# First x tiles of a two-branch kernel loaded and turned by pairs of 128-feature chunks, with extra warm-up matmuls and pinned parameter turns

## The chip, the cores and the metric

The kernel runs on one core of a Trainium2 chip. The metric is the device time of one execution in microseconds (us). PE is TensorE's matmul side, PEld its weight loads, DVE is VectorE, ACT is ScalarE, SP is the queue that issues most DMAs.

Three measures are used side by side: the timed runs; the profile's timeline of TensorE; and the completion records of the trace, which give for each DMA the moment at which each of the 16 DMA engines reported its share as landed. A time "landed at 15.03" is the last of the 16. All times inside a run count from the start of its span.

## The reference, cut to what matters

Two independent branches, each over 2048 tokens of 1024 features, are concatenated. Branch A is a complex state-space scan. Branch B is segment-wise attention of 32 heads with a memory carried from segment to segment. Only the start of B's value projection matters here:

```python
v = jnp.einsum('btd,dhe->bhte', h, Wv)      # h: (memory and) tokens x 1024, Wv: 1024 x 32 x 128
```

The kernel computes it in blocks of four heads (512 columns of Wv). The weights of block 0 are called wv0 below, those of block 1 wv1, 1 MB each.

## The kernel before: the parts that the change and the argument touch

The value matmuls of this kernel contract over the partitions, so x (tokens by features) must be turned to features by tokens. For the first 512 tokens this is done on TensorE (a matmul with the identity into a PSUM buffer, then a VectorE copy from there to SBUF); the other 1536 tokens use transposing loads. The split is meant to avoid transposing loads that arrive too late; the first of them was issued from 11.27 us in the kernel before and landed at 20.03. In the profile lines below a_hs is the SBUF buffer that x's rows and the weights are loaded to, b_xe holds the turned x, and psO, psS and psP are buffers in PSUM.

```python
    def load_rows(self, t, xr, e, cs=slice(0, D)):
        self.k.tc.keep_in_program_order(e.dma_start(xr[:, t, cs], self.x[0][t * 128 + 64:t * 128 + 192, cs]))

    def turn_rows(self, t, xr):
        k = self.k
        pt = k.ps("O", (128, 2, 1024), BF16)
        for c in range(KC):                                   # KC = 8 chunks of 128 features
            k.tc.keep_in_program_order(k.PE.transpose(pt[...], xr[:, t, c * 128:(c + 1) * 128], k.ident[:]))
        for i in range(2):
            k.copy("v", self.xe[:, 4 * i:4 * i + 4, t * 128:(t + 1) * 128], pt[:, i, 0:512]...)

    def v_first(self, w, xr, e):                              # block 0, tokens 0 to 511
        p = [k.ps("A") for t in range(4)]
        for t, todo in enumerate((((0, 0, 2),), ((0, 2, 4), (1, 0, 4)), ((0, 4, 6), (1, 4, 6), (2, 0, 6)),
                                  ((0, 6, 8), (1, 6, 8), (2, 6, 8), (3, 0, 8)))):
            self.turn_rows(t, xr)
            for tt, c0, c1 in todo:
                self.v_mm(p[tt], tt, w, range(c0, c1))        # 128 x 512 matmuls, one per chunk
        ...                                                   # evacuation by ScalarE, store
# ---- in kernel_main
            q2 = (k.SP, nc.scalar)                            # two issuing queues
            for t in range(4):
                for j in range(2):
                    b.load_rows(t, xr, q2[j], slice(j * 512, j * 512 + 512))      # 128 KB each
                for j in range(2):
                    b.load_wv(0, wvs[0], KC, q2[j], [2 * t + j])                  # 128 KB each
            for j in range(2):
                b.load_wv(1, wvs[1], 2, q2[j], [j])           # wv1: two halves of 512 KB
            a.load_params(tmp)                                # three loads of 2 KB
            k.SP.dma_start(tmp[0:M, 0:D], b.mem0[0])          # 16 KB
            b.load_x(512, 1024); b.load_x(1024, 1536); b.load_x(1536, T)          # transposing loads
            ...
            for i in range(7):                                # warm-up
                k.PE.matmul(pw[:, i % 2, :], one[:, 0:128], one, start=True, stop=True)
```

After block 0's four tiles TensorE goes on with the first four tiles of block 1, which need wv1; in the middle of them it turns the parameters (nine small matmuls). The loads take their completion semaphores in turn from a set of eight (numbers 100 and 103 to 109 here), and from the ninth load on each issue waits for the semaphore that it is to use, that is for the load eight before it. The ninth was issued at 3.42 us, the first had landed at 3.40.

## Time and profile before

| | before |
|---|---|
| time, median of all its runs in the first comparison | 1242.95 us (1242.38 to 1243.32, 6 runs) |
| span of the profiled run | 1240.8 us |
| PE busy | 1234.9 us |
| block 1 (wv1) starts | 15.07 us |
| last 32 matmuls start | 1235.23 us |

First the page: the span, and busy time (share of the span) and instructions of each engine. Then the list of who PE waited for in the whole run (total us, times, longest).

```profile
span 1240.8 us, 19711 instructions
...
PE 1234.9 (100%) x8148; PEld 655.2 (53%) x8148; DVE 611.2 (49%) x1124; ACT 325.9 (26%) x754; POOL 199.9 (16%) x284
```

```profile
PE psO L913 <- PEq L1118: 0.9, 1, 0.9
PE psO L379 <- DMA a_hs<-in_B_x_dram: 0.6, 1, 0.6
PE psS L414 <- DVE b_xe L77: 0.5, 1, 0.5
PE psS L414 <- DMA a_hs<-in_B_Wv_dram: 0.2, 1, 0.2
```

TensorE is the bottleneck, and all its listed waits lie in the first 15.1 us. The PE timeline of that stretch (start, busy time, line, operation, how many; in brackets the idle time before and what ended it; L379 are the turns, L414 the value matmuls; the last line, L718, is the kernel's last 32 matmuls):

```profile
3.79 1.06 PE L379 MATMUL psO<-ident,a_hs 128*128 128x128 bf16 x8
5.37 0.64 PE L414 MATMUL psS<-a_hs,b_xe 128*128 128x512 bf16 x2 [0.52 <-DVE b_xe L77]
6.59 0.62 PE L379 MATMUL psO<-ident,a_hs 128*128 128x128 bf16 x8 [0.58 <-DMA a_hs<-in_B_x_dram]
...
12.96 1.89 PE L414 MATMUL psP<-a_hs,b_xe 128*128 128x512 bf16 x8
15.07 1.90 PE L414 MATMUL psS<-a_hs,b_xe 128*128 128x512 bf16 x8 [0.22 <-DMA a_hs<-in_B_Wv_dram]
...
1235.23 1.95 PE L718 MATMUL psP<-b_xe,b_ol 128*128 128x128 bf16 x32
```

The 0.52 us is the wait for VectorE's copy of the first turned tile, the 0.58 us the wait for the second x tile. The last eight matmuls of block 0 start at 12.96 us; eight take 1.73 us (start to start), so block 0 is through at 14.69 us. Block 1 starts at 15.07 us. The completion records say why:

```
landed at (us)      x tile 0   wv0 c0,1   x tile 1   wv0 c2,3   x tile 2   wv0 c4,5   x tile 3   wv0 c6,7      wv1 halves
kernel before       3.59       4.92       6.55       7.28       7.82       8.58       9.52       11.42         15.03 (first), 14.84
```

wv1's first half lands 0.04 us before its first matmul. Between 9 and 10 us the DMAs move only 171 GB/s (332 between 5 and 7 us).

### The profile page before, as it was taken

What the parts mean: (1) busy time and instruction counts of PE and PEld (TensorE: products, weight loads), DVE (VectorE), ACT (ScalarE), POOL (GpSimd) and SP (SyncE); (2) the same over time, 40 slices, a digit from 0 to 9 for tenths busy, and PEclk for the clock granted to TensorE, in tenths of its full rate; (3) what the DMA queues carried; (4) which work ended last, traced back from release to release, by engine and by line L of the source; (5) the groups of instructions that cost most, each with busy time, mean ns of one, the idle gap of its engine ahead of it and who ended that gap; (6) DMA issues with size and microseconds to landing.
All of it is one profiled execution on the core that took longest, in us unless ns stands there. A gap on an engine that the chain in (4) does not pass through costs nothing.

```text
span 1240.8 us, 19711 instructions
## 1 busy us (share of the span) xinstructions
PE 1234.9 (100%) x8148; PEld 655.2 (53%) x8148; DVE 611.2 (49%) x1124; ACT 325.9 (26%) x754; POOL 199.9 (16%) x284
## 2 busy tenths in 40 slices
PE   9999999999999999999999999999999999999998
PEld 4444444444455445566666655655565554454444
DVE  4889999999941222444444444444444550011000
ACT  3344434444310001333333323333333230000000
POOL 2000000000032140222222222232222330000000
PEclk9999999999999999999999999999999999999999
DMA  9942232332566558577668554645575469607000
GB/s 223 260 130 68 85 94 68 102 94 77 153 189 202 158 161 170 100 151 150 138 122 173 123 136 95 129 77 103 106 139 106 72 203 231 140 18 153 17 18 28
DMA packets 306056, 153.95 MB, mean 124 GB/s; under 512 B 147242, under 2 KB 299810, under 8 KB 305962
## 3 DMA queue, kind: packets, MB, share of 16 engines
q1 hardware_dynamic: 304138, 150.82, 52.6%
q10 hardware_dynamic: 1824, 1.84, 0.5%
q8 instruction: 65, 1.06, 0.4%
q14 instruction: 29, 0.24, 0.1%
HBM read 73.70 MB, written 44.71 MB: 95 GB/s over the span
## 4 chain that ended last, share of the span: by engine, by line
PE 98%; DMA 1%; DVE 0%; issue 0%
PE psP L585 33%; PE psS L685 9%; PE psO L256 9%; PE psS L414 9%; PE psP L414 9%; PE psP L685 5%; PE psS L310 4%; PE psP L310 4%; PE psP L568 4%; PE psO L629 3%; PE psS L611 3%; PE psO L685 2%; PE psS L718 1%; PE psP L505 1%; PE psP L737 1%; PE psO L482 1%
## 5 line engine op out<-in xcount | busy, mean ns | idle before, releaser
L585 PE MATMUL psP<-b_xe,w 128*128 128x480 bf16 x2048 | 439.6, 366 | 0.0
L585 PEld LDWEIGHTS <-w 128*128 128x128 bf16 x2048 | 193.7, 98 | 183.5
L618 POOL TENSOR_TENSOR b_m<-b_e,maskB 99x396 bf16<-99x396 bf16 x160 | 139.4, 871 | 348.2 <-ACT b_e L614 348.2
L77 DVE CAST b_q<-psP 128x480 bf16<-128x480 f32 (+1 forms) x192 | 98.1, 532 | 145.4 <-PE psP L585 133.9
L414 PEld LDWEIGHTS <-b_xe 128*128 128x128 bf16 x1024 | 99.8, 98 | 121.3 <-DVE b_xe L77 1.1
L75 ACT ACTIVATE b_k<-psP 128x480 bf16<-128x480 f32 x128 | 73.1, 571 | 319.1 <-PE psP L585 319.1
L685 PEld LDWEIGHTS <-b_ol 128*128 128x128 bf16 x960 | 93.1, 98 | 109.3
L614 ACT ACTIVATE b_e<-psS 99x396 bf16<-99x396 f32 x176 | 87.4, 497 | 170.9 <-PE psS L611 165.5
L636 DVE TENSOR_TENSOR b_ot<-psO,b_rall 99x512 bf16<-99x512 f32 x176 | 121.7, 692 | 6.4
L256 PE MATMUL psO<-w,a_bt 128*128 128x512 bf16 x512 | 115.7, 379 | 0.0
L634 DVE RECIPROCAL b_rall<-psO 99x4 f32<-99x4 f32 x176 | 31.3, 178 | 132.8 <-PE psO L629 132.8
L685 PE MATMUL psS<-w,b_ol 128*128 128x512 bf16 x416 | 92.1, 379 | 0.0
L414 PE MATMUL psS<-w,b_xe 128*128 128x512 bf16 x384 | 90.7, 379 | 0.0
L414 PE MATMUL psP<-w,b_xe 128*128 128x512 bf16 x384 | 90.7, 379 | 0.0
L256 PEld LDWEIGHTS <-a_bt 128*128 128x128 bf16 x512 | 49.7, 98 | 59.0
L310 PEld LDWEIGHTS <-a_hs 128*128 128x128 bf16 x512 | 49.5, 98 | 58.3
L77 DVE CAST b_ost<-psS 128x512 bf16<-128x512 f32 x13 | 9.0, 692 | 125.4 <-PE psS L685 125.4
L629 PE MATMUL psO<-b_v,b_m 99*128 99x129 bf16 x704 | 70.4, 221 | 0.0
L611 PEld LDWEIGHTS <-b_k 128*128 128x128 bf16 x704 | 50.0, 98 | 33.9 <-DVE b_k L77 0.2
L611 PE MATMUL psS<-b_q,b_k 128*128 128x99 bf16 x704 | 60.1, 208 | 0.0
L75 ACT ACTIVATE b_vst<-psS 128x512 bf16<-128x512 f32 x56 | 33.4, 597 | 99.5 <-PE psS L414 75.6
L310 PE MATMUL psS<-w,a_hs 128*128 128x512 bf16 x256 | 57.9, 379 | 0.0
(203 smaller groups left out, 1097.9 us busy)
## 6 DMA issues: line engine op xcount, KB each, us to landing
b_v<-b_vx SPq DMA_DIRECT2D x16, 1056.0 KB
b_os<-b_ot SPq DMA_DIRECT2D x16, 960.0 KB
w<-in_B_Wv_dram SPq DMA_DIRECT2D x14, 1024.0 KB
b_vx<-b_vst SPq DMA_DIRECT2D x48, 256.0 KB
w<-in_B_Wo_dram SPq DMA_DIRECT2D x12, 1024.0 KB
w<-in_B_Wq_dram SPq DMA_DIRECT2D x16, 512.0 KB
w<-in_B_Wk_dram SPq DMA_DIRECT2D x16, 512.0 KB
a_xn<-in_A_x_dram SPq DMA_DIRECT2D x32, 128.0 KB
```

Of the source, the lines that this page charges most:

```text
L75: self.S.activation(out, in_, ACT.Copy)
L77: self.V.tensor_copy(out, in_)
L256: m = PE.matmul(u[:, i, :], self.bt[:, i, c, :], self.xT[tb][:, c, :], start=(c == 0), stop=(c == KC - 1))
L310: PE.matmul(py[:], self.hs[tb][:, pc, i, tt * 128:(tt + 1) * 128], self.ct[half, i][:, pc, :], start=(pc == 0 and i == 0), stop=(pc == PC ...
L414: m = self.k.PE.matmul(p[:], self.xe[:, c, t * 128:(t + 1) * 128], w[:, c, :], start=(c == 0), stop=(c == KC - 1))
L585: PE.matmul(p[:, 0:480], w[:, i * KC + c, hh * 128:(hh + 1) * 128], self.xe[:, c, 480 * q:480 * q + 480], start=(c == 0), stop=(c == KC - 1))
L611: PE.matmul(s[:, j * GW:(j + 1) * GW], kt[:, hh, g0:g0 + 128], qt[:, hh, g0:g0 + GW], start=True, stop=True)
L614: k.S.activation(e[:], s[0:GW, 0:4 * GW], ACT.Exp, scale=float(E) ** -0.5, accum_out=self.accE[0:GW, i:i + 1])
L618: k.G.tensor_tensor(v4(m[:, 0:4 * GW]), v4(e[:]), mask[0:GW, :, :].unsqueeze(2).to_broadcast([GW, 2, 2, GW]), ALU.mult)
L629: PE.matmul(o[:, gg, cs], m[:, j * GW:j * GW + 128], vt[:, 2 * u + gg, cs], start=True, stop=True)
L636: V.tensor_tensor(ot[:, 2 * u:2 * u + 2, :].rearrange("p g (h e) -> p g h e", h=2), oa[:, :, 1:257].rearrange("p g (h e) -> p g h e", h=2) ...
L685: k.PE.matmul(self.acc[t, half], ol[:, h8, tt * 128:(tt + 1) * 128], self.wo_half(half, h), start=(h == 0), stop=(h == H - 1))
```

## The change

Its intent: let TensorE start sooner and wait less in block 0. x comes in pieces of 256 tokens by 256 features (two chunks), each turned by four turns and one copy; the filler matmul of 384 columns covers the first copy; the warm-up is 256 columns longer. The turns of the parameters and of the initial memory get pins, so that the scheduler keeps them at their place in TensorE's order. Two side effects: each Wv chunk now goes to the queue that does not carry the x piece beside it, and the warm-up matmuls are pinned too and write to a psS buffer instead of psO.

```diff
-    def load_rows(self, t, xr, e, cs=slice(0, D)):
-        self.k.tc.keep_in_program_order(e.dma_start(xr[:, t, cs], self.x[0][t * 128 + 64:t * 128 + 192, cs]))
-    def turn_rows(self, t, xr):   # 8 turns, 2 copies (cut)
+    def load_rows(self, j, q, xr, e):
+        cs = slice(256 * q, 256 * q + 256)
+        self.k.tc.keep_in_program_order(e.dma_start(
+            xr[:, 2 * j:2 * j + 2, cs], self.x[0][256 * j + 64:256 * j + 320, cs].rearrange("(i p) d -> p i d", p=128)))
+    def turn_rows(self, j, q, xr, c0=0, n=2):   # 2 turns per chunk, 1 copy (cut)
@@ v_first
-        for t, todo in enumerate((((0, 0, 2),), ((0, 2, 4), (1, 0, 4)), ...)):   # cut
+        for c in range(2):
+            self.turn_rows(0, 0, xr, c, 1)
+        self.warm(384)
+        for q in range(4):
+            if q > 0:
+                self.turn_rows(1, q, xr)
+            for t in range(2):
+                self.v_mm(p[t], t, w, (2 * q,))
+            if q == 0:
+                self.turn_rows(1, q, xr)
+            for t in range(2):
+                self.v_mm(p[t], t, w, (2 * q + 1,))
+            if q < 3:
+                self.turn_rows(0, q + 1, xr)
+            for t in range(2, 4):
+                self.v_mm(p[t], t, w, range(2 * q, 2 * q + 2))
@@ kernel_main
-            for t in range(4):
+            for q in range(4):
                 for j in range(2):
-                    b.load_rows(t, xr, q2[j], slice(j * 512, j * 512 + 512))
-                for j in range(2):
-                    b.load_wv(0, wvs[0], KC, q2[j], [2 * t + j])
+                    b.load_rows(j, q, xr, q2[j])
+                    b.load_wv(0, wvs[0], KC, q2[1 - j], [2 * q + j])
-            for i in range(7):
-                k.PE.matmul(pw[:, i % 2, :], one[:, 0:128], one, start=True, stop=True)
+            for n in 7 * (512,) + (256,):
+                b.warm(n)                       # one pinned matmul of n columns; its definition is cut
@@ params, init
-        PE.matmul(pr[:, 0:3 * PC], r24, ...)
+        k.tc.keep_in_program_order(PE.matmul(pr[:, 0:3 * PC], r24, ...))          # and the same for mem0's turns
```

The bytes, the number of loads ahead of wv1 (16), the turns and the value matmuls are the same.

More of the change, by code (lines that the diff above doesn't have):

```diff
@@ L149, in params @@
         pr = k.ps("O")[:, 0, :]
-        PE.matmul(pr[:, 0:3 * PC], r24, k.ident[0:3 * PC, 0:3 * PC], start=True, stop=True)
+        k.tc.keep_in_program_order(PE.matmul(pr[:, 0:3 * PC], r24, k.ident[0:3 * PC, 0:3 * PC], start=True, stop=True))
         raw = pool.tile([128, 3, PC], FP32, name="a_raw", bufs=1)
@@ L343, in init @@
         for c in range(KC):
-            k.PE.matmul(pm[:, c * M:(c + 1) * M], tmp[0:M, c * 128:(c + 1) * 128], k.ident[0:M, 0:M], start=True, stop=True)
+            k.tc.keep_in_program_order(
+                k.PE.matmul(pm[:, c * M:(c + 1) * M], tmp[0:M, c * 128:(c + 1) * 128], k.ident[0:M, 0:M], start=True, stop=True))
         self.memT = self.xe[:, :, T:XE]
@@ L369, in load_x @@
                 k.SP.dma_start(self.xe[:, :, lo:hi], self.x[0][lo + r:hi + r, :], transpose=True)
-    def load_rows(self, t, xr, e, cs=slice(0, D)):
-        self.k.tc.keep_in_program_order(e.dma_start(xr[:, t, cs], self.x[0][t * 128 + 64:t * 128 + 192, cs]))
-    def turn_rows(self, t, xr):
-        k = self.k
-        pt = k.ps("O", (128, 2, 1024), BF16)
-        for c in range(KC):
-            k.tc.keep_in_program_order(k.PE.transpose(pt[:, c // 4, (c % 4) * 128:(c % 4) * 128 + 128], xr[:, t, c * 128:(c + 1) * 128], k.ident[:]))
-        for i in range(2):
-            k.copy("v", self.xe[:, 4 * i:4 * i + 4, t * 128:(t + 1) * 128], pt[:, i, 0:512].rearrange("p (c n) -> p c n", c=4))
+    def load_rows(self, j, q, xr, e):
[3 more added lines that the diff above has]
+    def turn_rows(self, j, q, xr, c0=0, n=2):
+        k = self.k
+        pt = k.ps("O", (128, 2, 256), BF16)
+        for c in range(n):
+            for i in range(2):
+                cs = 256 * q + 128 * (c0 + c)
+                k.tc.keep_in_program_order(k.PE.transpose(
+                    pt[:, c, i * 128:i * 128 + 128], xr[:, 2 * j + i, cs:cs + 128], k.ident[:]))
+        k.copy("v", self.xe[:, 2 * q + c0:2 * q + c0 + n, 256 * j:256 * j + 256], pt[:, 0:n, :])
     def sum_x(self, q, pool):
@@ L442, in v_pair, with warm @@
         yield
+    def warm(self, n):
+        k = self.k
+        one = k.nc.const_aps.tensor(1.0, [128, n], BF16)
+        k.tc.keep_in_program_order(k.PE.matmul(self.pw[:, 0, 0:n], one[:, 0:128], one, start=True, stop=True))
     def v_first(self, w, xr, e):
@@ L447, in v_first @@
         p = [k.ps("A") for t in range(4)]
-        for t, todo in enumerate((((0, 0, 2),), ((0, 2, 4), (1, 0, 4)), ((0, 4, 6), (1, 4, 6), (2, 0, 6)),
-                                  ((0, 6, 8), (1, 6, 8), (2, 6, 8), (3, 0, 8)))):
-            self.turn_rows(t, xr)
-            for tt, c0, c1 in todo:
-                self.v_mm(p[tt], tt, w, range(c0, c1))
+        for c in range(2):
[14 more added lines that the diff above has]
+                self.v_mm(p[t], t, w, range(2 * q, 2 * q + 2))
         for q in range(2):
@@ L909, in kernel_main @@
             b.load_x(1536, T)
-            one = nc.const_aps.tensor(1.0, [128, 512], BF16)
-            pw = k.ps("O")
-            for i in range(7):
-                k.PE.matmul(pw[:, i % 2, :], one[:, 0:128], one, start=True, stop=True)
+            b.pw = k.psp.tile([128, 1, 512], FP32, name="psS", bufs=2)
+            for n in 7 * (512,) + (256,):
+                b.warm(n)
             def values():
```

## The prediction

> **What bounds the kernel.** TensorE. The profile page has PE busy 1234.9 of 1240.8 us. The table of PE waits for the whole run lists four: 0.9 us before the first instruction, 0.6 us for a load of B's x, 0.5 us for VectorE's copy of the first turned tile, 0.2 us for Wv. All lie in the first 15.1 us. So the change can only move the moment from which PE runs without a gap: 15.07 us in the before timeline, where the second value block (weights wv1) starts.
>
> **What the change does.** Before, PE takes four 128-token tiles, 8 turns each; after, pieces of 256 tokens by 256 features (4 turns, one copy). Turns, matmuls and bytes stay the same. Added: 256 and 384 columns of warm-up. In the instruction order the pinned parameter turns keep their place on PE: worth 0.0 us. x loads become 512 B packets instead of 1024 B.
>
> **PE's side (estimate).** From the trace: a warm 512 matmul 0.216 us (8 in 1.73), a turn 0.055, cold 0.43 and 0.107; the copy of 512 columns 0.38 us. The first four turns start at 4.0 us (warm-up is 0.2 us longer), the filler hides the copies, the first value matmul starts about 4.8 instead of 5.37; a short wait for the second pieces at about 6.2 remains. v_first then ends near 13.6 us instead of 14.7: about 1.0 us gained. The clock should warm up at the same time (full rate from about 5.4 us before[...]).
>
> **DMA's side.** Completion records of the trace (last of 16 engines): x tile 0 at 3.6, wv0 chunks 0 and 1 at 4.9, x tile 1 at 6.55, chunks 2, 3 at 7.3, x tile 2 at 7.8, chunks 4, 5 at 8.6, x tile 3 at 9.5, chunks 6, 7 at 11.4, wv1's halves at 14.84 and 15.03. PE's 15.07 start is wv1's arrival: PE was already out of work at 14.7. The change doesn't touch wv1: it is issued behind the same 2 MB, with the same eight transfers in flight. So the 1.0 us becomes a longer wait for wv1 (about 1.3 us instead of 0.22).
>
> Smaller packets can make it later: median 27 ns per 512 B packet against 46 ns per 1024 B, so 1 MB of x costs (2048*27-1024*46)/16 = 0.5 us more engine time; DMA isn't saturated throughout (9 to 10 us moved only 171 GB/s), so I expect 0 to 0.4 us, against some luck in which engine straggles (wv0's last chunk had 15 of 16 engines done at 9.7 and the last at 11.25).
>
> **Critical path.** Of the 1.0 us on PE nearly nothing reaches the end. Expected: -0.7 to +0.5 us, centre -0.2 (0.1 by the DMA argument, shaded for a luckier landing of wv1).
>
> **Prediction.** 1242.9 us, 8 in 10 between 1242.1 and 1243.7; faster by over 2% 0.003, within 2% 0.994, slower 0.003.
>
> **What would show it.** Right: in the PE timeline the first block's matmuls end at 13 to 14 us; the waits list has a Wv wait over 1 us; the next block starts at 14.7 to 15.5; the copy wait is gone. Wrong: the second block starts before 14.3 us, or the first ends past 14.5.
>
> **What would make it wrong.** wv1 landing much earlier (fewer stragglers, or the x transposes of the SP queue starting later and contending less) would give up to 1.2 us; more contention[...] would cost 0.5 to 2 us.

That the clock would warm up at the same time as before (the trace's record has full rate from 5.48 us) was the estimate.

## The result, and the profile after

| | before | after |
|---|---|---|
| time, median (range, runs) | 1242.95 us (1242.38 to 1243.32, 6) | 1242.87 us (1241.89 to 1243.31, 6) |
| ratio, 95% interval | | 0.9999 (0.9986 to 1.0012) |
| block 0 through on PE | 14.69 | 13.93 |
| wv1's first half landed | 15.03 | 15.09 |
| block 1 starts | 15.07 | 15.13 |
| last 32 matmuls start | 1235.23 | 1235.30 |
| span | 1240.8 | 1240.9 |

Ratios are the mean time of one kernel's runs over that of the other's of the same rounds, so they are not quite the ratio of the medians. The page, the PE waits of the whole run, and the largest waits of the weight loads (PEld):

```profile
span 1240.9 us, 19646 instructions
...
PE 1231.7 (99%) x8080; PEld 655.7 (53%) x8150; DVE 611.2 (49%) x1125; ACT 326.2 (26%) x754; POOL 200.3 (16%) x284
```

```profile
PE psS L420 <- ACT a_hs L75: 1.0, 1, 1.0
PE psS L454 <- PEq L1139: 0.8, 1, 0.8
```

```profile
PEld L420 <- DMA a_hs<-in_B_Wv_dram: 1.5, 1, 1.5
```

(The trace of this run lacks 68 matmul records, 8080 against 8148; so its busy sum is not to be compared.) The PE timeline: L385 are the turns, L454 warm-up and filler, L420 the value matmuls, L741 the last 32 matmuls.

```profile
4.00 0.63 PE L385 MATMUL psO<-ident,a_hs 128*128 128x128 bf16 x4
4.43 0.53 PE L454 MATMUL psS<-const-bfloat16-1.0 128*128 128x384 bf16 x1
4.81 0.61 PE L420 MATMUL psS<-a_hs,b_xe 128*128 128x512 bf16 x1
...
13.50 0.59 PE L420 MATMUL psP<-a_hs,b_xe 128*128 128x512 bf16 x2
15.13 1.90 PE L420 MATMUL psS<-a_hs,b_xe 128*128 128x512 bf16 x8 [1.04 <-ACT a_hs L75]
...
1235.30 1.95 PE L741 MATMUL psP<-b_xe,b_ol 128*128 128x128 bf16 x32
```

Block 0 runs without the two waits of before and is through at 13.93 us (its last two matmuls start at 13.50 and take 0.216 us each), 0.76 us earlier. Then PE stands for 1.04 us (the timeline counts from the modelled end of the last matmul, 14.09 us) and starts block 1 at 15.13 us, as late as before. The timeline puts that wait down to ScalarE, the weight loads' list to the DMA of Wv. The records say the DMA: wv1's first half landed at 15.09 us.

### The profile page after: what moved, and what is told of

Its sections match the earlier page's. It is cut to its first block, busy times and chain, and to the rows that moved or that the text cites. A ratio compares the mean times of both kernels' runs of the same rounds, so it can differ in the third digit from the quotient of the medians.

```text
span 1240.9 us, 19646 instructions
## 1 busy us (share of the span) xinstructions
PE 1231.7 (99%) x8080; PEld 655.7 (53%) x8150; DVE 611.2 (49%) x1125; ACT 326.2 (26%) x754; POOL 200.3 (16%) x284
## 4 chain that ended last, share of the span: by engine, by line
PE 99%; issue 0%; ACT 0%; DVE 0%
PE psP L608 33%; PE psS L708 9%; PE psS L420 9%; PE psO L256 9%; PE psP L420 9%; PE psP L708 5%; PE psP L310 4%; PE psS L310 4%; PE psP L591 4%; PE psO L652 3%; PE psS L634 3%; PE psO L708 2%; PE psS L741 1%; PE psP L528 1%; PE psP L760 1%; PE psO L505 1%
## 5 line engine op out<-in xcount | busy, mean ns | idle before, releaser
L420 PEld LDWEIGHTS <-b_xe 128*128 128x128 bf16 x1024 | 99.7, 98 | 120.4 <-DMA a_hs<-in_B_Wv_dram 1.5
L420 PE MATMUL psS<-w,b_xe 128*128 128x512 bf16 x378 | 90.1, 379 | 0.4
L420 PE MATMUL psP<-w,b_xe 128*128 128x512 bf16 x376 | 89.8, 379 | 0.4
```

Of the source, the lines that this page charges most:

```text
L420: m = self.k.PE.matmul(p[:], self.xe[:, c, t * 128:(t + 1) * 128], w[:, c, :], start=(c == 0), stop=(c == KC - 1))
```

## The experiments

Every run's output was correct. Twelve kernels ran, all with five rounds, in three groups; the kernel before ran beside each group with medians of 1242.22 (11 runs), 1242.43 (9) and 1242.67 us (9). Because the intervals are about 0.0013 wide on either side (1.6 us), the timeline carries the verdicts. The table has for each profiled run when block 1 started, when the last 32 matmuls of the kernel started, the difference of the two, and what remained to the end of the span.

| run | loads ahead of wv1 | wv1 first half landed | block 1 starts | last 32 start | difference | rest to the end | DMAs against before |
|---|---|---|---|---|---|---|---|
| before | 16 | 15.03 | 15.07 | 1235.23 | 1220.16 | 5.60 | 0 |
| after | 16 | 15.09 | 15.13 | 1235.30 | 1220.17 | 5.60 | 0 |
| e1 after, no wv1 wait | 16 | (15.00) | 14.05 | 1234.29 | 1220.24 | | 0 |
| e2 before, no wv1 wait | 16 | (14.75) | 14.65 | 1234.79 | 1220.14 | | 0 |
| e3 after, late x | 16 | 15.46 | 15.50 | 1237.31 | 1221.81 | 6.13 | +1 |
| e4 after, fewer loads | 10 | 13.34 | 14.57 | 1234.72 | 1220.15 | 6.12 | -6 |
| e5 after, mixed loads | 12 | 14.50 | 14.54 | 1234.70 | 1220.16 | 5.91 | -4 |
| e6 before, mixed loads | 12 | 14.28 | 14.60 | 1234.75 | 1220.15 | 5.91 | -4 |
| e7 as e5, no extra warm-up | 12 | 13.89 | 14.30 | 1234.45 | 1220.15 | 5.91 | -4 |
| e8 after, no pins | 16 | 16.30 | 17.56 | 1239.00 | 1221.44 | 5.60 | 0 |
| e9 as e7, DMA count kept | 12 | 14.30 | 14.52 | 1234.67 | 1220.15 | 5.61 | 0 |
| e10 before, one DMA more | 16 | 15.78 | 15.83 | 1235.99 | 1220.16 | 6.14 | +1 |
| e11 before, mixed, count kept | 12 | 13.41 | 14.95 | 1235.11 | 1220.16 | 5.58 | 0 |
| e12 after, 11 loads, count kept | 11 | 13.80 | 14.97 | 1235.12 | 1220.15 | 5.56 | 0 |

The column "difference" is the main reading: except in e3 and e8 the work from block 1 to the last matmuls takes 1220.14 to 1220.24 us whatever the start was like. A gain or loss at 15 us arrives at the end of TensorE's work unchanged; nothing takes it back on the way.

Theory A: TensorE's gain in block 0 is eaten by the wait for wv1. Rival B: block 1 waits for ScalarE to free its PSUM bank, as the timeline's releaser says. Rival C: the gain is given back later.

### e1 and e2: block 1 without its wait for wv1

```diff
-                    yield from b.v_pair(hb, q, wvs[hb], k.SP)
+                    yield from b.v_pair(hb, q, wvs[0 if q < 2 else hb], k.SP)
```

The same edit in the changed kernel (e1) and in the one before (e2).

> The changed kernel, but the second value block's first four tiles multiply by the first block's weights (wrong result on purpose; every load stays, in the same order). Theory A (the gain on TensorE is eaten by the wait for wv1): the wait of 1.04 us at 15.1 us goes, PE runs without a gap from 13.9 us, and the kernel takes 1.0 to 1.2 us less than before: about 1241.8 us, ratio 0.999. Rival B (the new block waits for ScalarE's evacuation of its PSUM bank, as the profile's releaser names it): the wait stays and the time stays at 1242.9. Rival C (the gain is given back later, at the x tiles or the parameter chain): the wait at 15 us goes but another appears by 30 us, and the time stays at 1242.9.

> The same edit in the kernel before (wrong result on purpose). Theory A: only its 0.2 to 0.4 us of wv1 wait goes, so PE starts the second block at 14.7 us, 0.75 us later than the changed kernel does with this edit; time about 1242.6 us. Rival B: no change at all. Rival C: about the same as the changed kernel with this edit.

My expectation of the time was useless: the kernel checks its own result and, since the wrong weights made that check fail, took its slow general path, 13772.4 and 13773.3 us (and so a correct output). The main part still ran first and is in the trace. The first two lines are of e1's PE timeline, then two of e2's:

```profile
13.62 0.59 PE L420 MATMUL psP<-a_hs,b_xe 128*128 128x512 bf16 x2
14.05 1.89 PE L420 MATMUL psS<-a_hs,b_xe 128*128 128x512 bf16 x8
```

```profile
12.92 1.89 PE L414 MATMUL psP<-a_hs,b_xe 128*128 128x512 bf16 x8
14.65 1.89 PE L414 MATMUL psS<-a_hs,b_xe 128*128 128x512 bf16 x8
```

No wait is left in either. Block 1 starts 1.08 us earlier than in the changed kernel's own run, and the last 32 matmuls start 1.01 us earlier. Rival B falls: ScalarE's part was not touched, and the wait is gone. Rival C falls: the gain arrives at the end. The change's order is worth 14.65 - 14.05 = 0.60 us on TensorE in this pair, and it needs wv1 to be there. The end of block 0 says the same in more profiles: it came at 13.93, 14.05 and 13.92 us with the changed order and 16 loads (changed kernel, e1, e3), and at 14.69, 14.65 and 14.55 us with the order of before (before, e2, e10). So the order gains 0.5 to 0.8 us there. (e8 is left out: a late piece of x held it up.)

### e3: the transposing loads held until wv1 has landed

```diff
+            gd = k.drp.tile([1, 2], BF16, name="gd")
+            tc.keep_in_program_order(k.SP.dma_start(gd[:], w01[0:1, 4096 + 2047:4096 + 2049]))   # reads both halves of wv1
             b.load_x(512, 1024)      # and load_x's DMAs pinned behind it
```

> The changed kernel with the transposing loads of x columns 512 to 2047 held until wv1 has landed (a 4-byte copy that reads both halves of wv1 stands before them in the queue). If those loads' small packets are what delays wv1 (its first half lands at 15.09 us): wv1 lands at about 13.5 to 14.2 us, the second block starts there, 0.9 us gained, unless x's second 512 columns then land after 21 us, where PE would wait for them. If wv1 is late only because it was issued late (7.5 to 7.9 us): it lands at 14.7 to 15.1 as before and the time stays within 0.3 us of 1242.9.

Measured: 1244.09 us (1243.30 to 1246.54), ratio 1.0019 (1.0006 to 1.0031). wv1's halves landed at 15.46 and 14.44 us, although no transposing load ran beside them. So the gain that their contention would have had to give (wv1 at 13.5 to 14.2 us) did not come. This is one profile, and the last of the 16 DMA engines was late in it (15 had landed the first half by 14.68 us, in the changed kernel by 15.08), so a contention worth a few tenths of a us is not excluded. The held loads themselves became a new wait:

```profile
15.50 1.90 PE L420 MATMUL psS<-a_hs,b_xe 128*128 128x512 bf16 x8 [1.42 <-DMA a_hs<-in_B_Wv_dram]
...
23.22 1.90 PE L420 MATMUL psS<-a_hs,b_xe 128*128 128x512 bf16 x8 [0.22 <-DMA b_xe<-in_B_x_dram]
```

The 0.22 us is only part of the 1.65 us that this run loses after block 1 starts (difference 1221.81); its list of PE waits has another 0.9 us for ScalarE, which I did not trace further.

### e4: fewer loads ahead of wv1

```diff
-            for q in range(4):
-                for j in range(2):
-                    b.load_rows(j, q, xr, q2[j])
-                    b.load_wv(0, wvs[0], KC, q2[1 - j], [2 * q + j])
+            for j in range(2):
+                b.load_rows(j, 0, xr, q2[j])
+                b.load_wv(0, wvs[0], KC, q2[1 - j], [j])
+            for q in range(1, 4):
+                b.load_rows(0, q, xr, q2[q % 2], 4)            # 256 KB: all four tiles of a pair of chunks
+                b.load_wv(0, wvs[0], 4, q2[1 - q % 2], [q])    # 256 KB
```

> The changed kernel with 10 loads instead of 16 ahead of wv1 (the first pair of chunks as before, the other three pairs as one 256 KB load of x and one of Wv each). A load waits for the one eight before it; so wv1 may be issued when the third and fourth loads land (about 4.8 us) instead of 7.5. If the gap of DMA work from 9 to 10.5 us is what makes wv1 late: it lands 0.5 to 1.3 us earlier (13.8 to 14.6), and the second block starts then, time 1242.0 to 1242.5. If the transposing loads are the cause: these are issued earlier too, wv1 lands at 14.7 or later, and the time stays. Risk: the coarser pieces of x make PE wait inside the first block.

Measured: wv1 landed at 13.34 and 12.97 us, 1.7 us earlier, and the DMAs moved 333 and 336 GB/s in 8 to 10 and 10 to 12 us, against 229 and 296 in the changed kernel. So wv1 was late mainly because it was issued late (its half on ScalarE's queue at 7.22 us in the changed kernel, at 4.80 here). The other profiles agree: with 16 loads ahead its first half landed between 14.75 and 16.30 us (seven profiles), with 10 to 12 between 13.34 and 14.50 (seven). These edits make the loads ahead larger as well as fewer; no run separates the two. But the coarse second piece of x landed only at 7.13 us (the changed kernel's at 5.56 and 6.78), and PE waited for it:

```profile
7.18 0.40 PE L385 MATMUL psO<-ident,a_hs 128*128 128x128 bf16 x4 [0.66 <-DMA a_hs<-in_B_x_dram]
...
14.57 1.89 PE L420 MATMUL psS<-a_hs,b_xe 128*128 128x512 bf16 x8
```

Block 1 and the last 32 matmuls start 0.5 us earlier than before. Yet the time was 1242.18 us against 1242.22, ratio 1.0000 (0.9987 to 1.0013), and the span 1240.8 us as before: the rest after the last 32 matmuls was 6.12 us instead of 5.60.

### e5, e6 and e7: small pieces first, large loads later

```diff
+            for q in range(2):                                 # 8 loads of 128 KB, as in the changed kernel
+                for j in range(2):
+                    b.load_rows(j, q, xr, q2[j])
+                    b.load_wv(0, wvs[0], KC, q2[1 - j], [2 * q + j])
+            for q in range(2, 4):                              # 4 loads of 256 KB
+                b.load_rows(0, q, xr, q2[q % 2], 4)
+                b.load_wv(0, wvs[0], 4, q2[1 - q % 2], [q])
```

e6 does the same to the kernel before (x tiles 2 and 3 and their Wv chunks as 256 KB loads). e7 is e5 without `warm(384)` and without the warm-up of 256 columns.

> The changed kernel with 12 loads instead of 16 ahead of wv1: the first two pairs of chunks in small pieces as in the changed kernel (so that the 0.66 us wait for a coarse piece of x that the fewer-loads run showed goes), the last two pairs as one 256 KB load each. Theory: wv1 is late because it is issued late, behind the limit of eight loads in flight. wv1 should be issued at about 5.5 us instead of 7.5, land by 13.5, and PE should start the second block at about 13.9 to 14.0 us without a wait: 1.1 us earlier than before, and the last group of matmuls of the kernel 1.1 us earlier too (about 1234.1 us). Time about 1 us under before (ratio 0.9991); the interval may not separate that from zero. Rival (wv1 late because of contention or of the number of bytes): second block starts at 14.5 or later.

> The kernel before with the same 12 loads ahead of wv1 (first two x tiles and four Wv chunks in small pieces, the rest one 256 KB load each). If the change's new order is worth about 0.75 us on TensorE once wv1 is early: here PE still ends its first block at 14.6 to 14.8 us, the second starts there, gain 0.3 to 0.5 us over before, last group at about 1234.8 us. If the loads alone were the whole story: it starts the second block at 14.0 as the changed kernel with these loads does.

> The changed kernel with the mixed loads, without the change's two extra warm-up matmuls (256 and 384 columns). PE would idle about 0.2 us before the first turns and 0.4 us while the first chunk is copied. If the fillers matter only for keeping the clock's warming going: full-rate matmuls begin 0 to 1 us later than with them (at 6 to 7 us instead of about 5.9) and the second block starts 0 to 0.5 us later than in the mixed-loads run. If they cost time themselves: it starts up to 0.1 us earlier.

Measured, against 1242.43 us: e5 1242.40 us (1242.33 to 1244.25; 1.0008, 0.9994 to 1.0022), e6 1242.45 (1.0001, 0.9987 to 1.0014), e7 1242.15 (0.9999, 0.9986 to 1.0013). Block 1 started at 14.54, 14.60 and 14.30 us. e5 missed my 13.9 to 14.0: wv1 landed no earlier than 14.50, and before that PE waited 0.49 us for the last pair of x, whose load was now in flight together with wv1's (in e7, with the same loads, it was issued at 4.67 us and wv1's second half at 5.29). Two lines of e5, then one of e6:

```profile
11.33 0.40 PE L385 MATMUL psO<-ident,a_hs 128*128 128x128 bf16 x4 [0.49 <-DMA a_hs<-in_B_x_dram]
...
14.54 1.90 PE L420 MATMUL psS<-a_hs,b_xe 128*128 128x512 bf16 x8
```

```profile
14.60 1.89 PE L414 MATMUL psS<-a_hs,b_xe 128*128 128x512 bf16 x8
```

So e5, with the change, started block 1 no earlier than e6 without it (0.06 us apart). The sentence "the change is worth 0.75 us once wv1 is early" was not confirmed with real loads. Nor does this pair refute it: e5's block 0 was through at 14.38 us, and wv1 (14.50) still set the start.

e7 shows no cost of leaving out the extra warm-up matmuls. But the moment at which the clock's record goes to full rate was scattered over the 14 profiles, from 3.67 us (e12) to 6.76 (e2), with no visible relation to the added warm-up matmuls (3.67 to 6.40 us with them, 3.92 to 6.76 without). It came early in e7 (4.16 us; e5 5.63), so this says nothing for or against the fillers.

### e8: the changed kernel without the pins

```diff
-        k.tc.keep_in_program_order(PE.matmul(pr[:, 0:3 * PC], r24, ...))       # and the same for mem0's turns
+        PE.matmul(pr[:, 0:3 * PC], r24, ...)
```

> The changed kernel without the two pins on the parameter turns. Built so, the scheduler puts the nine small turns directly behind the first value block, where PE waits for wv1 for 1 us, instead of after the second block's third tile. If their inputs have landed by 13.9 us: the 0.3 us of turns fall into the wait, the second block still starts at 15.1 us, and everything after it is 0.3 us earlier (last group at about 1235.0 us). If their inputs land after 15.1 us, the second block starts later and the time grows.

Measured: 1245.20 us (1243.38 to 1246.31), ratio 1.0019 (1.0006 to 1.0033). Two lines of the PE timeline (L150 are the parameter turns), then two of the table of stretches (stretch, its length, busy time and instructions of PE, PEld, DVE, ACT, POOL, then granted clock, DMA share, GB/s):

```profile
17.09 0.17 PE L150 MATMUL psO<-ident,a_hs 24*128 24x24 bf16 x1 [1.55 <-DMA a_hs<-in_A_log_dt_dram]
...
17.56 2.99 PE L419 MATMUL psS<-a_hs,b_xe 128*128 128x512 bf16 x8
```

```profile
18.00:20.00 2.00, 2.00 (x7) 0.78 (x6) 1.83 (x14) 0.21 (x1) 0.00 (x0) 0.56 1.17 266
20.00:22.00 2.00, 2.00 (x7) 0.73 (x6) 2.00 (x5) 1.40 (x2) 0.00 (x0) 0.59 1.18 124
```

The scheduler puts the turns ahead of block 1, and their inputs, the last small loads in the queue, land there only at 17.0 us (16.1 in the changed kernel). TensorE waits for them, and then the clock falls to half: the records have it low from 18.22 to 21.63 us, and the eight matmuls from 17.56 us take 2.99 us instead of 1.90. PE had waited 1.87 us (for x, below) and 1.55 us before that, with work between; after a single wait of 1.42 us (e3) or 1.12 us (e10) the granted clock stayed at 1.00. These runs show no more than that of what makes the clock fall. Block 1 started 2.4 us later than in the changed kernel. Part of that is bad luck of this execution: its last pair of x landed at 13.36 us (10.92 in the changed kernel) and cost another 1.87 us of wait in block 0, and wv1 itself landed only at 16.30 us; the turns account for about 1.2 us, from there to 17.56. The pins remain necessary in the new order: even with the changed kernel's landing times, turns placed ahead of block 1 would have waited until 16.1 us, past its start at 15.13.

### e9 to e12: the end of the program, and what could beat both

The table's last two columns had shown that 4 or 6 DMAs fewer, or one more, cost 0.3 to 0.5 us after the last matmul. The trace has the reason to test. At the end SP checks the eight completion semaphores one after the other, about 0.07 us each; in the kernel before, the last output's is the eighth. Its sequence of checks in both kernels, by number of the semaphore:

```
before  100: 1238.12  103: 1238.22  104: .30  105: .38  106: .45  107: .53  108: .59  109: 1239.02 (last output landed 1239.01)
e4      102: 1237.84  103: 1238.52 (last output landed 1238.50)  104: .60  105: .68  106: .75  107: .83  108: .89  109: 1238.96
```

In e4 the output landed 0.51 us earlier, but six checks still followed. e9, e11 and e12 therefore restore the number of DMAs by cutting a copy of zeros in the middle of the kernel into more pieces; e10 adds one such piece to the kernel before and does nothing else, except that in all four the pieces now stand together behind the loop over which they were spread.

```diff
-            if hb < 6:
-                put(self.omd[NM:MT, (0, 1536, 2048, ...)[hb]:(1536, 2048, 2560, ...)[hb]], MT - NM)
+        cut = [0, 512, 1536, 2048, 2560, 3072, 3584, 4096]     # e10: 7 pieces for 6; e9, e11: 10; e12: 11
+        for lo, hi in zip(cut, cut[1:]):
+            put(self.omd[NM:MT, lo:hi], MT - NM)
```

e9 is e7 with this, e11 is e6 with this. e12 is the complete changed kernel with 11 loads ahead of wv1: x of the first two pairs in 128 KB pieces, everything after the first two Wv chunks in 256 KB loads.

> The changed kernel with the mixed loads and without the extra warm-ups (the run that started its second block earliest, 14.30 us), plus four more small zero copies in the middle (one load of zeros cut into more pieces) so that the number of DMAs in the kernel is that of before. Theory from the earlier traces: completion semaphores are taken in turn by eight; the end of the program checks them one after the other, 0.07 us each, and with four DMAs fewer the last output's semaphore is no longer the last one checked, which gave back 0.3 to 0.5 us. With the count restored, the time from the start of the last 32 matmuls to the end of the span is 5.6 us as before (5.95 without). Second block at 14.2 to 14.6 us, last group at 1234.4 to 1234.8, span 1240.0 to 1240.4, time 0.4 to 0.8 us under before. If the theory of the end is wrong: 5.9 to 6.0 us at the end again.

> The kernel before with one zero copy in the middle cut in two: one DMA more, nothing else. Theory of the end: the last output now uses the first semaphore in the order of the checks, so seven more checks follow its landing; the time from the last 32 matmuls to the end grows from 5.6 to about 6.0 to 6.1 us; second block at 15.0 to 15.1 us; span 1241.2 to 1241.4. Rival (the longer end of the earlier runs comes from something else, as the instruction fetch or chance): 5.6 us as before.

> The kernel before with the mixed loads and four more zero copies (count of DMAs as before). PE bound: second block at 14.6 to 14.8 us, last group at 1234.7 to 1234.9, end 5.6 us, span 1240.3 to 1240.5. If the changed order is worth anything once wv1 is early, the first run of this call starts its second block earlier than this one.

> The changed kernel complete, warm-ups and pins kept, with 11 loads ahead of wv1 (x of the first two pairs in 128 KB pieces, x of the last two and Wv from the second pair on in 256 KB loads) and five more zero copies, so the count of DMAs is that of before. wv1 issued at about 5 us, lands by 13.5; second block at 13.9 to 14.5 us (jitter of the slowest DMA engine decides), last group at 1234.1 to 1234.7, end 5.6 us, span 1239.7 to 1240.3, time 0.5 to 1.1 us under before. Rival: its loads of x or of wv1 arrive late and the second block starts at 14.6 or later, no better than the order of before with such loads.

Measured, against 1242.67 us: e9 1241.99 us (1241.73 to 1242.43; ratio 0.9993, 0.9980 to 1.0007), e10 1242.48 (0.9998, 0.9984 to 1.0012), e11 1242.48 (0.9997, 0.9983 to 1.0011), e12 1242.40 (0.9996, 0.9982 to 1.0010).

The theory of the end is confirmed: the rest was 5.61, 5.58 and 5.56 us with the count kept, and 6.14 us with one DMA more. In the timed runs 0.5 us is not visible, e10's least of all.

The start was not as I expected. e10 has the same start as the kernel before, instruction for instruction, and its block 1 began at 15.83 us:

```profile
15.83 1.90 PE L415 MATMUL psS<-a_hs,b_xe 128*128 128x512 bf16 x8 [1.12 <-DMA a_hs<-in_B_Wv_dram]
```

wv1's first half landed at 15.78 us there, at 15.03 and 14.75 us in the two other profiles with this start. And e12, where wv1 landed early (13.80 us), started block 1 only at 14.97 us, because pieces of block 0's own x and Wv came later:

```profile
9.75 0.40 PE L386 MATMUL psO<-ident,a_hs 128*128 128x128 bf16 x4 [0.69 <-DMA a_hs<-in_B_x_dram]
```

e12's third pair of x landed at 9.71 us (7.57 and 8.60 in the changed kernel), its load of wv0's chunks 2 and 3 at 7.99 us (5.18 and 6.66); PE waited 0.7 us for each of the two. With wv1 early, block 1 started at 14.57, 14.54, 14.30, 14.52 and 14.97 us with the changed order (e4, e5, e7, e9, e12), and at 14.60 and 14.95 us with the order of before (e6, e11). Two and a half megabytes must land before block 1 and the rest of wv1 soon after; in these runs either wv1 or a piece of block 0's own input was late. e9 is the only version whose five times lie almost wholly below those of the kernel before of the same rounds (1241.73 to 1242.43 against 1242.42 to 1243.87). It is the one to keep if any, but its interval still includes 1, so a gain is not shown.

## Why the prediction was right

- **The total.** Predicted 1242.9 us with 1242.1 to 1243.7; measured 1242.87 us. The mechanism, TensorE's gain turned into a longer wait for wv1, was right: e1 and e2 took the wait away and the gain appeared: block 1 started 1.08 us earlier in the changed kernel and 0.42 us earlier in the one before, so that the change was then 0.60 us ahead. That the number fits to 0.03 us is luck: the interval of the ratio is 1.6 us wide on either side, and the centre was the 1243.13 us of three earlier runs of the kernel before, less 0.2 us for a luck that did not come (last point).
- **"About 1.0 us gained" on PE.** The sign was right, the size too large: 0.76 us (14.69 to 13.93). Block 0 was predicted to end "near 13.6". The term that was mis-sized is the cold stretch: I let the clock warm up at the same time as before, but it went to full rate at 6.08 us instead of 5.48, so that the turns at 5.64 us still took 0.105 us each and the matmuls from 4.81 us about 0.4 us each. By estimate 0.6 us at half rate (a turn took 0.107 us before the change of rate and 0.056 after it, in the run before) is 0.3 us of work, which is the whole miss. That the clock came 0.6 us later is well inside the scatter of the profiles: full rate began 2.8 to 5.9 us after the first warm-up matmul in the 14 of them, so "at the same time" was not to be had. "A short wait for the second pieces at about 6.2 remains" was wrong: they had landed at 5.56 us.
- **"A longer wait for wv1 (about 1.3 us instead of 0.22)."** 1.04 us, smaller by the same 0.3 us.
- **wv1's landing, "0 to 0.4 us" later for the smaller packets.** 15.09 against 15.03 us. The packets did cost what was computed (27 ns for 512 B, 46 ns for 1024 B, medians of the changed kernel's first 12 us), but the DMAs were not saturated (229 GB/s in 8 to 10 us, where e4 moved 333), and the difference is far below the scatter of wv1's landing with an unchanged start (14.75 to 15.78 us; with the changed order 15.00, 15.09 and, in e8, 16.30).
- **Pins "worth 0.0 us".** Right as a comparison with before, since the position was the same; but e8 shows that without them the new order would have lost time. I had looked only at the instruction order of the finished change, not at what the scheduler does without that part of it.
- **What I did not see.** The centre was shaded to -0.2 us "for a luckier landing of wv1"; there was no such luck. Also missed was the reason for wv1's lateness: I named the bytes ahead of it and the loads in flight, but not that the limit of eight makes the late issue the cause (e4: 1.7 us earlier), nor that the transposing loads, which I named as a possible cause, are not the main one (e3).

What stays open: why the slowest of the 16 DMA engines differs so much from run to run (the last share of wv1's first half landed within a range of 1.0 us in three profiles with the start of before, 1.3 us in three with the changed one), how much of wv1's earlier landing comes from larger loads rather than fewer, whether the fillers help, and whether e9 gains anything in time.

## What to carry to other kernels

Before making a stage faster, look at what its successor waits for: a landing time just ahead of the first instruction after the stage is a wall; here no work inside the stage moved it (block 0 was through 0.76 us earlier, wv1 landed at 15.09 us against 15.03, block 1 started at 15.13 against 15.07). If a load is late, look at when it was issued and what its issue waited for before blaming bandwidth; fewer, larger loads ahead of it moved it here (from 15.09 to 13.34 us in e4), but a piece of block 0's own input then came later (e4, e5, e12). For gains below the scatter of the timed runs, compare the start of the same late instruction in two traces.
